# Linear attention into a swish MLP on one core: PSUM lent bank by bank, and the second batch's lead-in rearranged

## The chip, the cores and the metric

The kernel runs on one NeuronCore of one Trainium2 chip. The metric is device time in microseconds; a quoted time is the median of several executions. Each run also has a profile of one execution. The span in a profile is some 1.7 us shorter than the time of the same execution, because it goes from the first to the last instruction of the program. All runs here count as fast ones (with one core the only other label would be a run over 1.5% above the fastest).

## The reference

Two parts, one after the other, with 8 batches, 8 heads, 576 positions and head size 64:

```python
q_s = exp(q - max) / (sum over the head dimension + 1e-9)
k_s = exp(k - max) / (sum over the sequence + 1e-9)
kv  = einsum('bhsd,bhse->bhde', k_s, v)          # 64 x 64 for each head
x   = einsum('bhsd,bhde->bhse', q_s, kv)         # as 4608 tokens x 512
h   = x @ w_in                                   # 512 x 2048
g   = h * (1 / (1 + exp(-beta * h)))
out = g @ w_out                                  # 2048 x 512
```

The second part has nearly all the arithmetic: 1152 matmuls of 128x512 with a 128x128 weight, half of them for `h`, half for `out`.

## The kernel before

Tokens come in nine chunks of 512: one for each batch (its first 512 positions), and one of the eight batches' remaining 64 positions each. For a chunk, `h` is made in 16 units of four matmuls; ScalarE makes `th = tanh(beta*h/2)`, VectorE `g = (th + 1) * h`, and the second product (`acc`) takes `g` as its weight. From chunk 1 on, second-product matmuls stand between the units of the same chunk, four per unit and at least `LAG` units behind. The attention part of batch n+1 is hooked into chunk n. Batches 0 and 1 cannot be hidden so; each has a lead-in of its own, and the second lies between chunk 0 and chunk 1. For each pair of heads j, the lead-in has five `kv` matmuls, a norm (VectorE takes a reciprocal, then writes the kv blocks as `kvp`), one `x` matmul of 128x512 that needs the norm, and a copy of `x` out of PSUM. The units of `h` need all four.

```python
ldp = tc.tile_pool(name="ld", bufs=13)                 # landing buffers of all loads
psH = tc.tile_pool(name="psH", bufs=3, space=PSUM)     # h; also acc 2 and 3 of chunk 0
psB = tc.tile_pool(name="psB", bufs=2, space=PSUM)     # acc
psX = tc.tile_pool(name="psX", bufs=2, space=PSUM)     # transposes, x
psK = tc.tile_pool(name="psK", bufs=1, space=PSUM)     # kv
# [...]
def lead_in(b, fill):
    v_first(b, 0)
    v_cast(b, 0, nc.gpsimd); v_cast(b, 1, nc.gpsimd)
    v_cast(b, 2, nc.scalar); v_cast(b, 3, nc.scalar if b else nc.vector)
    fill(0)
    kv_mm(b, 0); kv_mm(b, 1)
    v_first(b, 1, 0, 1)
    v_cast(b, 4, nc.gpsimd); v_cast(b, 5, nc.scalar)
    kv_norm(b, 0, 2, nc.scalar)                        # half of it on ScalarE
    if b == 0:
        kv_mm(b, 2)
    fill(1)
    x_mm(b, 0); x_mm(b, 1)
    v_first(b, 1, 1, 2)
    v_cast(b, 6, nc.gpsimd); v_cast(b, 7, nc.scalar)
    if b:
        fill(2)
        kv_mm(b, 2)
    kv_norm(b, 2, 1, nc.vector)
    x_out(b, 0, nc.scalar); x_out(b, 1, nc.scalar)
    fill(3)
    kv_mm(b, 3)
    x_mm(b, 2)
    kv_norm(b, 3, 1, nc.vector)
    # [... x_out 2, x_mm 3, x_out 3 ...]
    for i in range(2 + b):
        unit_mm(b, i, 0, 3)                            # first three quarters of 2 or 3 units

def loads_1():
    for hf in range(2): load_q(1, hf)
    load_w_out(12); load_w_out(14)
    for hf in range(2): load_kv("k", k, 1, hf, True)
    load_kv("v", v, 1, 0, True)
    load_kv("v", v, 1, 1, True, 0, 2); load_kv("v", v, 1, 1, True, 2, 4)
    # [... batch 2 ...]

for n in range(NCH):
    for i in range(NJ):
        unit_a(n, i, 3 if n < 2 and i < 2 + n else 0)
        for f in hooks.get((n, i), []): f()
        if n:
            b_mm(2 if n == 1 and i < 4 else 4)         # up to so many second-product matmuls
    if n == 0:
        b_mm(28)
        # [... q of batch 1: exp, sum, division ...]
        cast_w_out(12, nc.scalar); cast_w_out(14, nc.scalar)
        # [... exp of k ...]
        q_t_pe(1, 0, 0, 4, nc.vector)                  # 8 transposes, copied out by VectorE
        b_mm(8)
        q_t_pe(1, 1, 0, 4, nc.vector)
        b_mm(8)
        lead_in(1, lambda m: b_mm((0, 4, 4, 4, 0)[m]))
```

So chunk 0 has 64 second-product matmuls. Of these 56 are done before chunk 1, and the last eight between its first units.

The softmax here doesn't subtract the row's maximum and nothing guards it: scores larger than these inputs give would overflow.

## Time and profile before

| | before |
|---|---|
| time at first, median of 3 | 296.31 us (296.21 to 296.71) |
| the profiled execution | 296.77 us, span 295.1 us |
| TensorE busy | 95% of the span |
| pitch of 128x512 matmuls back to back | 0.216 us |

The page of the kernel before, its span, the line of busy times (busy us, share, instructions) and the engine line of the chain that ended last (shares of the span):

```profile
span 295.1 us, 4168 instructions
...
PE 280.9 (95%) x1421; PEld 131.2 (44%) x1449; DVE 162.2 (55%) x308; ACT 172.2 (58%) x281; POOL 75.6 (26%) x129
...
PE 80%; DMA 10%; DVE 4%; POOL 2%; ACT 1%; issue 1%; POOLq 0%; ACTq 0%; DVEq 0%
```

TensorE is the bound (busy 95% of the span), so time can be saved only where TensorE has nothing to do. The timeline of TensorE, from 20 to 70 us, shows where that is (start us, duration us, engine, line, operation, out<-in, how often; in brackets the idle time before and what ended it):

```profile
20.10 11.38 PE L350 MATMUL h<-xT,w_in_b 128*128 128x512 bf16 x51 [0.42 <-DVE g L364]
31.32 6.35 PE L393 MATMUL acc<-w_out_b,g 128*128 128x512 bf16 x27
40.14 0.62 PE L200 MATMUL tp<-ident,Eq 128*128 128x128 bf16 x8 [2.47 <-POOL Eq L183]
...
45.49 0.67 PE L271 MATMUL kv<-va,Ek 128*128 128x130 bf16 x9 [0.77 <-POOL va L143]
...
51.11 0.39 PE L312 MATMUL x<-qT,kvp 128*128 128x512 bf16 x1 [0.81 <-DVE kvp L292]
51.34 2.52 PE L350 MATMUL h<-xT,w_in_b 128*128 128x512 bf16 x9
...
61.40 1.02 PE L350 MATMUL h<-xT,w_in_b 128*128 128x512 bf16 x4 [0.74 <-DVE g L364]
...
64.42 1.03 PE L350 MATMUL h<-xT,w_in_b 128*128 128x512 bf16 x4
...
68.82 0.73 PE L271 MATMUL kv<-va,Ek 128*128 128x130 bf16 x10 [0.65 <-DVE kvp L292]
```

The brackets are a little short, since the ends of matmuls are modelled (2.47 us in the second one). In this text a gap is the time from one start to the next less the usual pitch: the second bracket is then 2.6 us. Small waits are in no bracket at all. The line at 64.42 is unit 9 of chunk 1.

The wait at 45.49 names GpSimd's casts of v. GpSimd itself waited for the load, as its own timeline shows:

```profile
44.68 1.25 POOL L143 TENSOR_SCALAR_AFFINE_SELECT va<-v 128x256 bf16<-128x256 f32 x3 [4.59 <-DMA v<-in_v_dram]
```

### The profile page before, as it was taken

The numbers are of one execution on the slowest core, as the hardware profiler recorded it, in microseconds if no ns is written. First come the engines' busy times: TensorE is split into PE (matmuls) and PEld (weight loads), VectorE is DVE, ScalarE is ACT, GpSimd is POOL, SyncE is SP. The second block draws the span as 40 slices with busy tenths as digits, with TensorE's granted clock in tenths as the row PEclk, the third lists the DMA queues.
The fourth block names the chain that finished last, engine by engine and source line by source line (L and its number), as shares of the span: only waits on it lengthen the run. The fifth ranks groups of instructions, "written<-read, shape, count | busy, mean of one in ns | idle before, by whom it ended". The sixth has DMA issues, their size and how long they took to land.

```text
span 295.1 us, 4168 instructions
## 1 busy us (share of the span) xinstructions
PE 280.9 (95%) x1421; PEld 131.2 (44%) x1449; DVE 162.2 (55%) x308; ACT 172.2 (58%) x281; POOL 75.6 (26%) x129
## 2 busy tenths in 40 slices
PE   8899967989999999999999999999999999999994
PEld 3444433434445444544454445444444444444441
DVE  5848474586677556655765476548544443343300
ACT  4568475784784568556864686458554544454511
POOL 8476622180082016200621063105300000000000
PEclk9999999999999999999999999999999999999999
DMA  7999999639939962995299419921400110031111
GB/s 239 357 384 386 370 340 355 245 84 300 258 99 265 338 63 93 281 330 65 75 257 361 75 71 236 369 57 71 109 25 13 71 39 36 0 72 38 36 71 71
DMA packets 54966, 51.67 MB, mean 175 GB/s; under 512 B 21136, under 2 KB 46752, under 8 KB 54944
## 3 DMA queue, kind: packets, MB, share of 16 engines
q1 hardware_dynamic: 54912, 51.39, 58.5%
q8 instruction: 11, 0.18, 0.3%
q14 instruction: 11, 0.09, 0.1%
q10 hardware_dynamic: 32, 0.01, 0.0%
HBM read 38.28 MB, written 9.44 MB: 162 GB/s over the span
## 4 chain that ended last, share of the span: by engine, by line
PE 80%; DMA 10%; DVE 4%; POOL 2%; ACT 1%; issue 1%; POOLq 0%; ACTq 0%; DVEq 0%
PE acc L393 38%; PE h L350 36%; DMA wi<-in_moe_w_in_dram 4%; DMA q<-in_q_dram 4%; PE kv L271 3%; DMA v<-in_v_dram 3%; PE x L312 2%; DVE va L448 1%; DVE g L364 1%; ACT th L362 1%; POOL Eq L183 1%; PE warm L459 1%; DVE kvp L292 0%; DVE qz L179 0%; PE tp L200 0%
## 5 line engine op out<-in xcount | busy, mean ns | idle before, releaser
L364 DVE SCALAR_TENSOR_TENSOR g<-th,h 128x512 bf16<-128x512 bf16 x144 | 98.4, 685 | 103.1 <-ACT th L362 102.9
L362 ACT ACTIVATE th<-h,beta_h 128x512 bf16<-128x512 f32 x144 | 98.9, 688 | 93.5 <-PE h L350 91.8
L393 PE MATMUL acc<-w_out_b,g 128*128 128x512 bf16 x557 | 143.9, 379 | 0.9
L350 PE MATMUL h<-xT,w_in_b 128*128 128x512 bf16 x506 | 129.1, 379 | 1.9 <-DVE g L364 1.2
L350 PEld LDWEIGHTS <-w_in_b 128*128 128x128 bf16 x576 | 56.3, 98 | 70.1 <-issue 2.8
L393 PEld LDWEIGHTS <-g 128*128 128x128 bf16 x576 | 55.2, 98 | 63.2 <-issue 1.3
L183 POOL TENSOR_TENSOR Eq<-Eq,qz 128x512 bf16<-128x512 bf16 (+1 forms) x26 | 29.0, 1114 | 97.2 <-DVE qz L180 70.5
L410 ACT ACTIVATE o<-acc 128x512 f32<-128x512 f32 x34 | 20.3, 596 | 9.9 <-PE acc L393 9.9
L241 ACT ACTIVATE Ek<-k 128x640 bf16<-128x640 f32 (+1 forms) x28 | 22.7, 810 | 2.6 <-DMA k<-in_k_dram 2.6
L179 DVE TENSOR_REDUCE qz<-Eq 128x8 f32<-128x512 bf16 (+1 forms) x28 | 21.2, 758 | 3.6 <-ACT Eq L171 3.6
L171 ACT ACTIVATE Eq<-q 128x512 bf16<-128x512 f32 (+1 forms) x28 | 19.3, 690 | 6.5 <-DMA q<-in_q_dram 6.5
L143 POOL TENSOR_SCALAR_AFFINE_SELECT va<-v 128x256 bf16<-128x256 f32 x56 | 21.0, 414 | 7.7 <-DMA v<-in_v_dram 7.6
L350 PE MATMUL h<-xTt,w_in_b 128*128 128x512 bf16 x62 | 16.2, 379 | 0.1
L271 PE MATMUL kv<-va,Ek 128*128 128x130 bf16 x160 | 12.0, 219 | 1.5 <-POOL va L143 0.8
L271 PEld LDWEIGHTS <-Ek 128*128 128x128 bf16 x160 | 10.1, 97 | 7.0 <-issue 4.5
L312 PE MATMUL x<-qT,kvp 128*128 128x512 bf16 x32 | 11.8, 380 | 1.2 <-DVE kvp L292 0.8
L459 PE MATMUL warm<-zero 128*128 128x512 bf16 x39 | 11.3, 437 | 1.3 <-DVE zero L421 1.3
L134 ACT CAST xT<-x 128x512 bf16<-128x512 f32 (+1 forms) x20 | 10.6, 540 | 2.4 <-DVE xT L148 2.2
L148 DVE CAST xT<-x 128x512 bf16<-128x512 f32 (+1 forms) x16 | 9.9, 618 | 0.1
L225 POOL TENSOR_TENSOR Et<-Et,zt 128x512 bf16<-128x512 bf16 x4 | 4.2, 1043 | 22.3 <-ACT th L362 11.3
L292 DVE TENSOR_TENSOR kvp<-kv,rk 64x128 bf16<-64x128 f32 (+1 forms) x34 | 9.3, 273 | 0.9
L143 POOL TENSOR_SCALAR_AFFINE_SELECT w_in_b<-wi 128x1024 bf16<-128x1024 f32 (+1 forms) x9 | 8.5, 948 | 4.7 <-DMA wi<-in_moe_w_in_dram 4.7
(43 smaller groups left out, 74.2 us busy)
## 6 DMA issues: line engine op xcount, KB each, us to landing
k<-in_k_dram SPq DMA_DIRECT2D x28, 320.0 KB, 6.5
v<-in_v_dram SPq DMA_DIRECT2D x26, 320.0 KB, 7.6
q<-in_q_dram SPq DMA_DIRECT2D x16, 512.0 KB, 5.1
out_dram<-o SPq DMA_DIRECT2D x32, 256.0 KB, 2.4
wi<-in_moe_w_in_dram SPq DMA_DIRECT2D x8, 512.0 KB, 7.8
wo<-in_moe_w_out_dram SPq DMA_DIRECT2D x8, 512.0 KB, 12.2
k<-in_k_dram SPq DMA_DIRECT2D x4, 256.0 KB, 7.5
qt<-in_q_dram SPq DMA_DIRECT2D x8, 128.0 KB, 8.5
```

What stands on the lines that cost most here:

```text
L143: nc.gpsimd.affine_select(out=dst, in_=src, pattern=[[0, n]], base=0, channel_multiplier=0, compare_op=ALU.is_equal, fill=fill0,)
L171: nc.scalar.activation(Eq[b][:, :, h0:h1, :].rearrange("p t h d -> p h t d"), ld["q", b, hf][:, a : a + h1 - h0, :].rearrange("p h (t d) - ...
L179: nc.vector.tensor_reduce(qz[b][:, :, h], Eq[b][:, :, h, :], axis=AX.X, op=ALU.add)
L183: eng.tensor_tensor(Eq[b][:, t0:t1, h0:h1], Eq[b][:, t0:t1, h0:h1], qz[b][:, t0:t1, h0:h1].unsqueeze(3).to_broadcast((P, t1 - t0, h1 - h0, ...
L241: nc.scalar.activation(Ek[b][:, :, h0:h1, :].rearrange("p t h d -> p h t d"), ld["k", b, hf][:, a : a + h1 - h0, :].rearrange("p h (t d) - ...
L271: nc.tensor.matmul(kvs[b, j // 2][:, j % 2, :], Ek[b][:, t, 2 * j : 2 * j + 2, :].rearrange("p h d -> p (h d)"), va[b % 2][:, t, j, :], st ...
L312: nc.tensor.matmul(xps[b, j][:], kvp[b][:, j, :], qT[b][:, :, j, :], start=True, stop=True)
L350: nc.tensor.matmul(hs[n, i][:], w_in_b[:, kt, i * P : (i + 1) * P], rhs_a(n, kt), start=(kt == 0), stop=(kt == KT - 1),)
L362: nc.scalar.activation(th[:], h[:], ACTF.Tanh, scale=beta_h[:, i : i + 1])
L364: nc.vector.scalar_tensor_tensor(out=g[:], in0=th[:], scalar=1.0, in1=h[:], op0=ALU.add, op1=ALU.mult)
L393: nc.tensor.matmul(acc[n, st][:], gs[n, j][:, st * P : (st + 1) * P], w_out_b[:, j, :], start=(j == 0), stop=(j == NJ - 1),)
L410: nc.scalar.activation(o[:], acc[n, st][:], ACTF.Copy, scale=0.5)
```

## The change

Its intent: give each PSUM bank a name and lend it to whichever stage needs one; do more of chunk 0's second product before the transposes of batch 1 (44, then 4) and leave sixteen of them, not eight, for the first units of chunk 1; do kv of pairs 2 and 3 before the x that do not need them (`lead_in` is shared, so batch 0 gets the new order too); write norm 0 wholly on VectorE, and move a few casts and copies to another engine; and load the last quarter of w_out behind k and v of batch 1. The idle matmuls (`spare`, on zeros) take the place of useful ones in the lead-in.

```diff
-    psH = [... 3 bufs ...]  psB = [... 2 ...]  psX = [... 2 ...]  psK = [... 1 ...]
+    banks = {n: [... a pool of one bank ...] for n in ("H0", "H1", "H2", "A0", "A1", "X0", "X1", "K")}
+    def h_bank(n, i):
+        if n == 0 and i < 12:
+            return ("H0", "H1", "H2", "A0", "A1")[i % 5]
+        if n == 1 and i < 2:
+            return ("X0", "H1")[i]
+        return f"H{(n * NJ + i) % 3}"
 [... acc of chunk 0 in A0, A1, X1, K; of the others in A0, A1 ...]
-    def lead_in(b, fill):
+    def lead_in(b, kb, xb, fill):
 [...]
-        kv_norm(b, 0, 2, nc.scalar)
-        if b == 0:
-            kv_mm(b, 2)
+        v_first(b, 1, 1, 2, nc.scalar)
+        v_cast(b, 6, nc.gpsimd)
+        v_cast(b, 7, nc.scalar)
+        kv_mm(b, 2, kb[1])
+        kv_norm(b, 0, 2)
         fill(1)
-        x_mm(b, 0)
-        x_mm(b, 1)
-        [... v_first, v_cast 6 and 7, fill(2), kv_mm 2 ...]
-        kv_norm(b, 2, 1, nc.vector)
+        x_mm(b, 0, xb[0])
+        kv_mm(b, 3)
+        x_mm(b, 1, xb[1])
+        kv_norm(b, 2, 1)
         x_out(b, 0, nc.scalar)
         x_out(b, 1, nc.scalar)
-        fill(3)
-        kv_mm(b, 3)
-        x_mm(b, 2)
-        kv_norm(b, 3, 1, nc.vector)
+        fill(2)
+        x_mm(b, 2, xb[2])
+        kv_norm(b, 3, 1)
 [...]
-        for i in range(2 + b):
+        for i in range(2 - b):
             unit_mm(b, i, 0, 3)
 [... loads_1: load_w_out(12), load_w_out(14) moved behind the loads of v ...]
-                b_mm(2 if n == 1 and i < 4 else 4)
+                b_mm(0 if n == 1 and i < 1 else 4)
         if n == 0:
-            b_mm(28)
+            b_mm(44)
 [... the casts of w_out 12 and 14 moved from here (ScalarE) to behind the lead-in (GpSimd) ...]
-            q_t_pe(1, 0, 0, 4, nc.vector)
-            b_mm(8)
-            q_t_pe(1, 1, 0, 4, nc.vector)
-            b_mm(8)
-            lead_in(1, lambda m: b_mm((0, 4, 4, 4, 0)[m]))
+            q_t_pe(1, 0, nc.vector, "X0")
+            b_mm(4)
+            q_t_pe(1, 1, nc.vector, "H2")
+            spare = bank("H0", [P, CH], F32, "spare")
+            def idle_1(m):
+                for _ in range((3, 2, 1, 1)[m]):
+                    nc.tensor.matmul(spare[:], zero[:, 0:P], zero[:], start=True, stop=True)
+            lead_in(1, ("H1", "X0"), ("H2", "H1", "X0", "H2"), idle_1)
```

The parts hang together. With w_out's last quarter loaded last, none of the sixteen matmuls that need it can stand in the lead-in, so they must wait for chunk 1. And with acc 2 and 3 of chunk 0 in the h pool, as before, they cannot wait: a deadlock. By the code, the two open accumulators hold two of three h buffers while the lead-in takes three for its first units. This is what the lent banks are for, and it is why the deferral alone could not be tried on the old layout.

More of the change, by code (lines that the diff above doesn't have):

```diff
@@ L52, with bank @@
     osp = ctx.enter_context(tc.tile_pool(name="os", bufs=4))
-    psH = ctx.enter_context(tc.tile_pool(name="psH", bufs=3, space=bass.MemoryType.PSUM))
-    psB = ctx.enter_context(tc.tile_pool(name="psB", bufs=2, space=bass.MemoryType.PSUM))
-    psX = ctx.enter_context(tc.tile_pool(name="psX", bufs=2, space=bass.MemoryType.PSUM))
-    psK = ctx.enter_context(tc.tile_pool(name="psK", bufs=1, space=bass.MemoryType.PSUM))
+    banks = {
+        n: ctx.enter_context(tc.tile_pool(name=f"ps{n}", bufs=1, space=bass.MemoryType.PSUM))
+        for n in ("H0", "H1", "H2", "A0", "A1", "X0", "X1", "K")
+    }
+    def bank(n, shape, dtype, name):
+        return banks[n].tile(shape, dtype, tag=n, name=name)
     ctx.enter_context(tc.manual_schedule())
@@ L77, with xbank @@
     ld: dict = {}
+    turn = [0]
+    def xbank(n=None):
+        turn[0] ^= 1
+        return n or f"X{turn[0]}"
     def unit(name):
@@ L191, in q_t_alloc, with q_t_pe @@
         qT[b] = atn.tile([P, NT, HP, P], BF16, tag="qT", name=f"qT{b}")
-    def q_t_pe(b, hf, t0, t1, eng):
+    def q_t_pe(b, hf, eng, n=None):
         if b not in qT:
             q_t_alloc(b)
-        ps = psX.tile([P, t1 - t0, 2, P], BF16, tag="x", name=f"tp{b}_{hf}_{t0}")
-        for t in range(t0, t1):
+        ps = bank(xbank(n), [P, NT, 2, P], BF16, f"tp{b}_{hf}")
+        for t in range(NT):
             for j in range(2):
@@ L200, in q_t_pe @@
                 nc.tensor.transpose(
-                    ps[:, t - t0, j, :],
+                    ps[:, t, j, :],
                     Eq[b][:, t, h : h + 2, :].rearrange("p h d -> p (h d)"),
@@ L204, in q_t_pe @@
                 )
-        cast(eng, qT[b][:, t0:t1, 2 * hf : 2 * hf + 2, :], ps[:])
+        cast(eng, qT[b][:, :, 2 * hf : 2 * hf + 2, :], ps[:])
     def q_t_dma(b):
@@ L245, in k_exp, with v_first @@
         )
-    def v_first(b, hf, j0=0, j1=2):
-        nc.vector.tensor_scalar(
-            va[b % 2][:, 0, 2 * hf + j0 : 2 * hf + j1, 0 : 2 * D].rearrange(
-                "p j (two d) -> p j two d", two=2
-            ),
-            ld["v", b, hf][:, 2 * j0 : 2 * j1, 0:D].rearrange("p (j two) d -> p j two d", two=2),
-            even[:, 0:1], None, op0=ALU.mult,
-        )
+    def v_first(b, hf, j0=0, j1=2, eng=None):
+        dst = va[b % 2][:, 0, 2 * hf + j0 : 2 * hf + j1, 0 : 2 * D].rearrange(
+            "p j (two d) -> p j two d", two=2
+        )
+        src = ld["v", b, hf][:, 2 * j0 : 2 * j1, 0:D].rearrange("p (j two) d -> p j two d", two=2)
+        if eng is nc.scalar:
+            nc.scalar.activation(dst, src, ACTF.Copy, scale=even[:, 0:1])
+        else:
+            nc.vector.tensor_scalar(dst, src, even[:, 0:1], None, op0=ALU.mult)
     def v_cast(b, h, eng):
@@ L264, with kv_mm @@
     kvs: dict = {}
-    def kv_mm(b, j):
-        if j % 2 == 0:
-            pool, tag = (psB, "acc") if b == 0 and j else (psK, "kv")
-            kvs[b, j // 2] = pool.tile([P, 2, VW], F32, tag=tag, name=f"kv{b}_{j}")
+    def kv_mm(b, j, n="K"):
+        if (b, j // 2) not in kvs:
+            t = bank(n, [P, 2, VW], F32, f"kv{b}_{j}")
+            kvs[b, j // 2] = t
         for t in range(K5):
@@ L306, with x_mm @@
     xps: dict = {}
-    def x_mm(b, j):
+    def x_mm(b, j, n=None):
         if b not in xT:
             xT[b] = atn.tile([P, KT, NT, P], BF16, tag="xT", name=f"xT{b}")
-        xps[b, j] = psX.tile([P, NT, P], F32, tag="x", name=f"x{b}_{j}")
+        xps[b, j] = bank(xbank(n), [P, NT, P], F32, f"x{b}_{j}")
         nc.tensor.matmul(
@@ L323, in x_tail @@
     def x_tail(b, eng):
-        ps = psX.tile([P, HP, R], F32, tag="x", name=f"xt{b}")
+        ps = bank(xbank(), [P, HP, R], F32, f"xt{b}")
         i = (b % 2) * R
@@ L344 @@
     hs: dict = {}
+    def h_bank(n, i):
[4 more added lines that the diff above has]
+        return f"H{(n * NJ + i) % 3}"
     def unit_mm(n, i, k0, k1):
         if k0 == 0:
-            hs[n, i] = psH.tile([P, CH], F32, tag="h", name=f"h{n}_{i}")
+            hs[n, i] = bank(h_bank(n, i), [P, CH], F32, f"h{n}_{i}")
         for kt in range(k0, k1):
@@ L390, in b_mm @@
             if j == 0:
-                pool, tag = (psH, "h") if n == 0 and st > 1 else (psB, "acc")
-                acc[n, st] = pool.tile([P, DM], F32, tag=tag, name=f"acc{n}_{st}")
+                name = (f"A{st % 2}", ("A0", "A1", "X1", "K")[st])[n == 0]
+                acc[n, st] = bank(name, [P, DM], F32, f"acc{n}_{st}")
             nc.tensor.matmul(
@@ L453 @@
         nc.gpsimd.memset(kvp[b][:], 0.0)
-    warm = psB.tile([P, CH], F32, tag="acc", name="warm")
+    warm = bank("H2", [P, CH], F32, "warm")
     def dummy(m, n=CH):
@@ L469 @@
     k_exp(0, 4, 8)
-    q_t_pe(0, 0, 0, 4, nc.vector)
+    q_t_pe(0, 0, nc.vector)
     dummy(3)
-    q_t_pe(0, 1, 0, 4, nc.vector)
-    bt = psH.tile([P, NJ], F32, tag="h", name="bt")
+    q_t_pe(0, 1, nc.vector)
+    bt = bank("H1", [P, NJ], F32, "bt")
     nc.tensor.transpose(bt[:], beta_r[:], identf[:])
@@ L484, in lead_in @@
         v_cast(b, 2, nc.scalar)
-        v_cast(b, 3, nc.scalar if b else nc.vector)
+        v_cast(b, 3, nc.vector)
         fill(0)
-        kv_mm(b, 0)
+        kv_mm(b, 0, kb[0])
         kv_mm(b, 1)
@@ L491, in lead_in @@
         v_cast(b, 5, nc.scalar)
-        kv_norm(b, 0, 2, nc.scalar)
-        if b == 0:
-            kv_mm(b, 2)
-        fill(1)
-        x_mm(b, 0)
-        x_mm(b, 1)
-        v_first(b, 1, 1, 2)
+        v_first(b, 1, 1, 2, nc.scalar)
         v_cast(b, 6, nc.gpsimd)
         v_cast(b, 7, nc.scalar)
-        if b:
-            fill(2)
-            kv_mm(b, 2)
-        kv_norm(b, 2, 1, nc.vector)
+        kv_mm(b, 2, kb[1])
+        kv_norm(b, 0, 2)
+        fill(1)
+        x_mm(b, 0, xb[0])
+        kv_mm(b, 3)
+        x_mm(b, 1, xb[1])
+        kv_norm(b, 2, 1)
         x_out(b, 0, nc.scalar)
         x_out(b, 1, nc.scalar)
-        fill(3)
-        kv_mm(b, 3)
-        x_mm(b, 2)
-        kv_norm(b, 3, 1, nc.vector)
-        x_out(b, 2, nc.vector, 0, 2)
-        x_out(b, 2, nc.scalar, 2, 4)
+        fill(2)
+        x_mm(b, 2, xb[2])
+        kv_norm(b, 3, 1)
+        x_out(b, 2, nc.vector)
         if b == 0:
@@ L515, in lead_in @@
             cast_w_in(0, 0, nc.gpsimd, 128, 256)
-        fill(4)
-        x_mm(b, 3)
-        x_out(b, 3, nc.vector, 0, 2)
-        x_out(b, 3, nc.scalar, 2, 4)
-        for i in range(2 + b):
+        fill(3)
+        x_mm(b, 3, xb[3])
+        x_out(b, 3, nc.scalar, 0, 2)
+        x_out(b, 3, nc.vector, 2, 4)
+        for i in range(2 - b):
             unit_mm(b, i, 0, 3)
@@ L525, in loads_1 @@
             load_q(1, hf)
-        load_w_out(12)
-        load_w_out(14)
         for hf in range(2):
@@ L532, in loads_1 @@
         load_kv("v", v, 1, 1, True, 2, 4)
+        load_w_out(12)
+        load_w_out(14)
         for hf in range(2):
@@ L537, in loads_1 @@
             load_kv("v", v, 2, hf)
-    lead_in(0, lambda m: dummy((2, 3, 2, 2, 2)[m]))
+    lead_in(0, ("K", "A0"), ("X0", "X1", "A1", "H1"), lambda m: dummy((1, 3, 1, 1)[m]))
     cast_w_in(256, 0, nc.gpsimd)
@@ L589 @@
         for i in range(NJ):
-            unit_a(n, i, 3 if n < 2 and i < 2 + n else 0)
+            unit_a(n, i, 3 if n < 2 and i < 2 - n else 0)
             for f in hooks.get((n, i), []):
@@ L602 @@
             q_div(1, 0, NT, nc.vector, 4, 8)
-            cast_w_out(12, nc.scalar)
-            cast_w_out(14, nc.scalar)
             for hf in range(2):
                 k_exp(1, 4 * hf, 4 * hf + 4)
-            q_t_pe(1, 0, 0, 4, nc.vector)
-            b_mm(8)
-            q_t_pe(1, 1, 0, 4, nc.vector)
-            b_mm(8)
-            lead_in(1, lambda m: b_mm((0, 4, 4, 4, 0)[m]))
+            q_t_pe(1, 0, nc.vector, "X0")
[4 more added lines that the diff above has]
+                for _ in range((3, 2, 1, 1)[m]):
+                    nc.tensor.matmul(
+                        spare[:], zero[:, 0:P], zero[:], start=True, stop=True
+                    )
+            lead_in(1, ("H1", "X0"), ("H2", "H1", "X0", "H2"), idle_1)
+            cast_w_out(12, nc.gpsimd)
+            cast_w_out(14, nc.gpsimd)
     b_mm(10000)
```

## The prediction

> **What bounds it now.** TensorE: the page has it 95% busy, and 80% of the chain of waits. In the timeline 128x512 matmuls start every 0.216 us, and from 70 us on almost without gaps, so only the start can shrink. Its gaps there: 0.6 us at 20.1 (h waits for g: three h banks), 2.6 at 40.1 (transposes wait for the division), 0.9 at 45.5 (kv waits for cast v), 0.3 at 47.1, 1.0 at 51.1, 0.2 at 52.0 (x waits for kvp, h for x), 0.2, 0.3, 0.9 at 58 to 61.4 (h waits for g; ScalarE is behind), 0.8 at 68.8 (second kv waits for the one K bank). From 31 us on: 7.2 us.
>
> **What the change does.**
> 1. Banks. [...] Chunk 0's h gets five for units 0 to 11, then three. The gap at 20.1 goes. But h12 takes h10's bank and waits for g10, which in the trace ends 1.6 us after its h, with one unit (0.86 us) between: a new gap of 0.8 us. Lead-in 0 is about even (norm all on VectorE saves a hop, h1 waits for x3's bank). The first h stage ends near 31.6, not 31.3.
> 2. 44 second-product matmuls (9.5 us) before the transposes, not 28, end at 41.1, after the division (40.1): the 2.6 us gap is filled.
> 3. Loads. The DMA view shows 345 to 390 GB/s up to 45 us: bandwidth-bound, 1.36 us per 512 KB. [...] Two w_out units out of the way bring batch 1's last v to 43.5, not 46.2. Then VectorE's queue (q out, v, v) sets the first kv, near 44.2.
> 4. Lead-in 1. Norm 0 ends about 46.0; the other two norms follow each other on VectorE (0.66 us each), and x2 waits for both, as its bank is theirs: x2 at 48.1, h of chunk 1 at 49.2 (51.3 before). Seven idle matmuls replace sixteen useful ones here.
> 5. So eight more chunk-0 matmuls (1.7 us) are left: of 2.1 us only 0.4 is net yet. They go, four per unit, into units 1 to 4 of chunk 1, where ScalarE (tanh 0.69 + exp 0.62 us per unit) starved TensorE: the 1.4 us of gaps at 58 to 61 and that at 52 should close. Net at unit 9, where both have done 73 second-product matmuls: 62.4 against 64.4.
> 6. Afterwards the same work in the same order; the gap at 68.8 stays. Moved copies and casts cost nothing.
>
> **Sum.** 2.0 us saved. Predicted **294.2 us**, 8 in 10 within **293.2 to 295.3**. Faster by over 2%: 0.01; within 2%: 0.98; slower: 0.01.
>
> **What would show it.** Right: no TensorE gap at 40; one of 0.8 before h12 near 28; last v near 43.5; a gap under 1.5 us before x2; none above 0.3 between units 1 and 9 of chunk 1; all after 70 shifted by 2 us. Wrong: v not earlier, TensorE waiting for GpSimd's casts in lead-in 1, or h waiting for g in chunk 1.
>
> **What would make it wrong.** The first h stage losing or gaining more; the kv, norm, x chain of lead-in 1 being longer; w_out's casts too late for units 1 to 4; ScalarE still behind in chunk 1.

## The result, and the profile after

| | before | after |
|---|---|---|
| time, median | 296.26 us (4 runs) | 294.65 us (4 runs) |
| ratio | | 0.9947 (95%: 0.993 to 0.9964) |
| the same again, later (chip 11) | 296.15 us (11 runs) | 294.60 us (6 runs), 0.9939 (0.9917 to 0.996) |
| the profiled execution | 296.77 us, span 295.1 us | 294.75 us, span 293.0 us |

A ratio is taken over the fast runs of both kernels in the same rounds, so it is not quite the ratio of the medians. The change saves 1.6 us by the medians, 0.5%. That is within 2%, as the prediction had it with 0.98, and clear of noise, since the interval ends at 0.9964. The two profiled executions differ by 2.0 us, mainly because that of before was itself 0.5 us slower than its median.

The page after, the same lines:

```profile
span 293.0 us, 4194 instructions
...
PE 283.7 (97%) x1453; PEld 131.7 (45%) x1453; DVE 162.0 (55%) x309; ACT 168.9 (58%) x274; POOL 77.4 (26%) x131
...
PE 82%; DMA 14%; DVE 2%; issue 1%; ACT 0%; POOL 0%; SPq 0%; ACTq 0%; POOLq 0%
```

TensorE's timeline after, from 20 to 70 us:

```profile
28.17 3.61 PE L368 MATMUL h<-xT,w_in_b 128*128 128x512 bf16 x16 [0.64 <-DVE g L382]
31.62 9.66 PE L411 MATMUL acc<-w_out_b,g 128*128 128x512 bf16 x44
41.12 0.61 PE L210 MATMUL tp<-ident,Eq 128*128 128x128 bf16 x8
...
44.31 1.01 PE L282 MATMUL kv<-va,Ek 128*128 128x130 bf16 x15 [0.63 <-DVE va L265]
...
48.05 0.39 PE L323 MATMUL x<-qT,kvp 128*128 128x512 bf16 x1 [1.02 <-DVE kvp L303]
...
49.23 1.89 PE L368 MATMUL h<-xT,w_in_b 128*128 128x512 bf16 x8 [0.35 <-DVE xT L158]
...
62.39 1.03 PE L368 MATMUL h<-xT,w_in_b 128*128 128x512 bf16 x4
...
66.79 0.73 PE L282 MATMUL kv<-va,Ek 128*128 128x130 bf16 x10 [0.66 <-DVE kvp L303]
```

Unit 9 of chunk 1 starts at 62.39 instead of 64.42; as many second-product matmuls (73) have been done by then in both. After that the two run alike. All that TensorE lost between 16 us and 70 us, in gaps as defined above:

| where | before | after |
|---|---|---|
| chunk 0: start of its units (17 to 20 us) | 0.8 | 0.4 |
| chunk 0: unit 12 (28 us) | 0 | 0.8 |
| first second-product matmuls (32 us) | 0.15 | 0 |
| transposes wait for the division (40 us) | 2.6 | 0 |
| first kv | 0.9 | 0.8 |
| x0 waits for norm 0 | 0.3 | 0.3 |
| the last x wait for norms 2 and 3 | 1.0 | 1.2 |
| h of chunk 1 waits for x | 0.2 | 0.5 |
| h waits for g (58 to 61 us) | 1.5 | 0 |
| second kv of batch 2 | 0.8 | 0.8 |
| idle matmuls in lead-in 1 | 0 | 1.5 |
| sum | 8.2 | 6.3 |

The sums differ by 1.9 us; h of chunk 0 starting at 16.58 and not 16.73 makes it 2.0. This table says where TensorE stood still. It does not say which part of the change is worth what, since a gap that is filled in one place can just be a later start in another. That is what the experiments are for.

VectorE's timeline after shows what now sets lead-in 1: the copy of the second transpose, then the v instructions (the two waited-for ones are the lines at 43.68 and 44.18), and later two norms in a row (46.64 to 48.00), for which x2 at 48.05 waits:

```profile
43.08 0.69 DVE L158 COPY qT<-tp 128x1024 bf16<-128x1024 bf16 x1 [0.62 <-PE tp L210]
43.68 0.58 DVE L265 TENSOR_SCALAR va<-v,even 128x256 bf16<-128x256 f32 x1
44.18 0.28 DVE L158 CAST va<-v 128x256 bf16<-128x256 f32 x1
...
46.64 0.17 DVE L293 RECIPROCAL rk<-kv 128x1 f32<-128x1 f32 x1 [0.77 <-PE kv L282]
46.85 0.46 DVE L303 TENSOR_TENSOR kvp<-kv,rk 64x64 bf16<-64x64 f32 x2
47.34 0.17 DVE L293 RECIPROCAL rk<-kv 128x1 f32<-128x1 f32 x1
47.54 0.46 DVE L303 TENSOR_TENSOR kvp<-kv,rk 64x64 bf16<-64x64 f32 x2
```

GpSimd's casts of v, for comparison with the line of before (44.68), begin 2.5 us earlier:

```profile
42.13 0.75 POOL L153 TENSOR_SCALAR_AFFINE_SELECT va<-v 128x256 bf16<-128x256 f32 x2 [1.83 <-DMA v<-in_v_dram]
```

### The profile page after: what moved, and what is told of

Its sections match the earlier page's. It is cut to its first block, busy times and chain, and to the rows that moved or that the text cites. A ratio compares the mean times of both kernels' runs of the same rounds, so it can differ in the third digit from the quotient of the medians.

```text
span 293.0 us, 4194 instructions
## 1 busy us (share of the span) xinstructions
PE 283.7 (97%) x1453; PEld 131.7 (45%) x1453; DVE 162.0 (55%) x309; ACT 168.9 (58%) x274; POOL 77.4 (26%) x131
## 4 chain that ended last, share of the span: by engine, by line
PE 82%; DMA 14%; DVE 2%; issue 1%; ACT 0%; POOL 0%; SPq 0%; ACTq 0%; POOLq 0%
PE acc L411 39%; PE h L368 37%; DMA v<-in_v_dram 5%; DMA wo<-in_moe_w_out_dram 4%; DMA wi<-in_moe_w_in_dram 3%; PE kv L282 3%; PE x L323 2%; DMA q<-in_q_dram 2%; DVE kvp L303 1%; POOL va L153 0%; PE xt L338 0%; DVE xT L158 0%; ACT th L380 0%; DVE g L382 0%; DVE rk L293 0%
## 5 line engine op out<-in xcount | busy, mean ns | idle before, releaser
L411 PE MATMUL acc<-w_out_b,g 128*128 128x512 bf16 x576 | 145.9, 379 | 0.0
L144 ACT CAST xT<-x 128x512 bf16<-128x512 f32 (+1 forms) x18 | 9.9, 557 | 5.7 <-PE x L323 5.7
L303 DVE TENSOR_TENSOR kvp<-kv,rk 64x128 bf16<-64x128 f32 (+1 forms) x36 | 9.9, 274 | 0.9
```

The costliest lines, as they stand in the source:

```text
L411: nc.tensor.matmul(acc[n, st][:], gs[n, j][:, st * P : (st + 1) * P], w_out_b[:, j, :], start=(j == 0), stop=(j == NJ - 1),)
```

## The experiments

The theory is that of the prediction: the chain division, transpose, copy, kv, norm, x sets the start of chunk 1, the load order keeps data out of this chain, and deferred matmuls fill TensorE where ScalarE is behind. Its rivals: the gain is the filled gap at 40 us; or the loads alone; or the order of pairs. All twelve kernels gave correct results. Edits are against the changed kernel if nothing else is said. A difference in us is between medians; kernels of different calls ran on different chips, and the ratio to the kernel before of the same rounds is given for each.

| run | median us | ratio to before (95%) |
|---|---|---|
| after_again | 294.60 | 0.9939 (0.9917 to 0.996) |
| e1_old_load_order | 295.41 | 0.9972 (0.9959 to 0.9984) |
| e2_no_idle | 295.58 | 0.997 (0.9942 to 0.9997) |
| e3_h12_bank | 293.82 | 0.9917 (0.9903 to 0.993) |
| e5_x2_bank | 293.96 | 0.9915 (0.99 to 0.993) |
| e6_useful_fill | 293.18 | 0.9894 (0.988 to 0.9907) |
| e7_two_per_unit | 293.99 | 0.992 (0.9907 to 0.9934) |
| e8_no_deferral | 294.89 | 0.9951 (0.993 to 0.9972) |
| e12_old_pair_order | 295.16 | 0.9968 (0.9939 to 0.9996) |
| e13_v_before_copy | 293.90 | 0.9919 (0.9896 to 0.9942) |
| c1_all_three | 292.00 | 0.985 (0.9832 to 0.9869) |
| c2_all_four | 291.85 | 0.9844 (0.982 to 0.9869) |

### after_again: the changed kernel once more

No edit; it gives a value on the chip of the last three experiments, and a look at how often its clock dips.

> The changed kernel once more, on the chip of the three runs beside it, so that they are compared on one chip: about 294.65 us; runs with a mean granted clock of 0.994 or less, if any, some 1.6 us longer.

Measured: 294.60 us; 294.43 to 294.83 in six executions, all with a mean granted clock of 0.998 or more.

### e1_old_load_order: is it the loads?

```diff
         for hf in range(2):
             load_q(1, hf)
+        load_w_out(12)
+        load_w_out(14)
 [... k, v ...]
-        load_w_out(12)
-        load_w_out(14)
```

> The changed kernel with only the load order of before (w_out's last quarter ahead of k, v of batch 1; casts stay behind the lead-in). Theory (the first kv of batch 1 is set by v's landing in this order): last v lands near 46.3 us instead of 43.6, first kv waits for GpSimd's cast of v, the chain of lead-in 1 is 1.4 us later, time about 296.05 us, +1.4 on the changed kernel. Rival (the order of matmuls and the banks made the whole gain; the loads are hidden): within 0.3 us of the changed kernel.

Measured: 295.41 us, 0.8 us more than the changed kernel. The mechanism is the expected one: in TensorE's timeline the kv now wait for GpSimd's casts.

```profile
44.05 0.22 PE L282 MATMUL kv<-va,Ek 128*128 128x130 bf16 x1 [0.40 <-DVE va L265]
44.94 0.95 PE L282 MATMUL kv<-va,Ek 128*128 128x130 bf16 x14 [0.68 <-POOL va L153]
```

The size was little more than half. The expectation took the landing times from the changed kernel's profile. In this execution all loads came earlier: the first half of q of batch 1 landed at 34.66 us, against 35.63 in the changed kernel's profile (landing times are read from the traces' transfer records). The same load landed at 35.42, 35.45, 35.05 and 34.85 in the profiles of before, e3, e6 and e7. Every slice of before's DMA view from 3 to 45 us has the DMA engines nine tenths busy or more. A landing time 30 us into such a start moved by a microsecond from one execution to another (34.66 to 35.63 us), and an estimate that adds a wait to one landing time inherits that.

### e3_h12_bank: the new gap at unit 12

```diff
         if n == 0 and i < 12:
             return ("H0", "H1", "H2", "A0", "A1")[i % 5]
+        if n == 0:
+            return ("H2", "H0", "H1", "H2")[i - 12]
```

> The changed kernel with units 12 to 15 of chunk 0 on banks H2, H0, H1, H2, so that unit 12 no longer takes the bank of unit 10. Theory: the 0.8 us gap before h12 goes, and since lead-in 1 is set by TensorE's and VectorE's queue and not by data, all of it reaches the end: about 293.9 us, -0.75. Rival (v's landing sets lead-in 1): the gain is eaten by a longer wait before the first kv, within 0.2 us of the changed kernel.

Measured: 293.82 us, 0.8 us less than the changed kernel; the gap is gone and the second product starts at 30.85 instead of 31.62. In this profile the h units of chunk 0 run through, with no bracket:

```profile
26.75 4.26 PE L370 MATMUL h<-xT,w_in_b 128*128 128x512 bf16 x19
30.85 2.32 PE L413 MATMUL acc<-w_out_b,g 128*128 128x512 bf16 x10
```

All of it reached the end, so v's landing did not set lead-in 1. This entry of the bank table costs 0.8 us for no gain.

### e6_useful_fill: is the filled gap at 40 us the gain?

```diff
-            b_mm(44)
+            b_mm(37)
 [...]
-                for _ in range((3, 2, 1, 1)[m]):
-                    nc.tensor.matmul(spare[:], zero[:, 0:P], zero[:], start=True, stop=True)
+                b_mm((3, 2, 1, 1)[m])
```

> The changed kernel with 37 instead of 44 second-product matmuls before the transposes, and the other seven in place of the seven idle ones. Theory: what counts is when the chain division, transpose, copy, kv, norm, x starts; a gap of about 0.75 us opens again before the transposes, the transposes start at 40.35 instead of 41.12 and all of chunk 1 comes 0.75 us earlier: about 293.9 us. Rival (filling the gap at 40 us was the gain): the reopened gap costs, +0.7 us or no change at best.

Measured: 293.18 us, 1.5 us less. Seven matmuls at 0.216 us are 1.5 us, and the chain came 1.2 us (transposes) to 1.4 us (kv, h) earlier. TensorE's timeline of this run, against 41.12, 44.31 and 49.23 in the changed kernel:

```profile
39.92 0.61 PE L210 MATMUL tp<-ident,Eq 128*128 128x128 bf16 x8
...
42.88 1.01 PE L282 MATMUL kv<-va,Ek 128*128 128x130 bf16 x15 [0.40 <-DVE va L265]
...
47.79 1.46 PE L368 MATMUL h<-xT,w_in_b 128*128 128x512 bf16 x6 [0.35 <-DVE xT L158]
```

The expected 0.75 us of reopened gap did not appear, as q had landed 0.6 us earlier in this execution (35.05 us) and the division was over in time. So the run shows one thing: work moved ahead of the transposes is not gained when it delays them. With 44, the changed kernel overfills: it puts work before the transposes, and idle matmuls behind them. It does not put the rival out, since with 37 the gap at 40 us stayed filled: what the other nine additional matmuls are worth there was not tried, and no run leaves the gap open in the new layout.

### e7_two_per_unit: does chunk 1 need four deferred matmuls per unit?

```diff
-                b_mm(0 if n == 1 and i < 1 else 4)
+                b_mm((0 if i < 1 else 2 if i < 9 else 4) if n == 1 else 4)
```

> The changed kernel with two second-product matmuls per unit instead of four in units 1 to 8 of chunk 1. Theory (the deferred matmuls fill the time in which ScalarE starves TensorE): gaps before h with waits for g come back in units 4 to 9, together about 0.9 us (0.5 to 1.4), and TensorE's total grows by that: about 295.5 us. Rival (ScalarE is not behind any more, since the lead-in is shorter): no gaps, within 0.2 us of the changed kernel.

Measured: 293.99 us, 0.65 us less, where 0.9 us more was expected. One small gap (0.17 us) came into the units; and the gap before the second kv of batch 2, 0.8 us in the changed kernel and in before, fell to 0.08:

```profile
63.00 0.73 PE L282 MATMUL kv<-va,Ek 128*128 128x130 bf16 x10
63.56 1.03 PE L411 MATMUL acc<-w_out_b,g 128*128 128x512 bf16 x4
64.43 1.03 PE L368 MATMUL h<-xT,w_in_b 128*128 128x512 bf16 x4
65.37 0.74 PE L282 MATMUL kv<-va,Ek 128*128 128x130 bf16 x10
```

In the changed kernel the sixteen are used up after unit 4. At the kv only one second-product matmul is far enough behind (`LAG`) to be let in, and one unit and one matmul do not cover the norm that the second kv waits for. With two per unit, some are still there: four stand between the two kv groups, and the norm is covered. So two per unit are enough for ScalarE, and the rest is worth more later.

### e8_no_deferral: eight deferred, as before, instead of sixteen

Against e1_old_load_order (w_out must be there early for this):

```diff
+            cast_w_out(12, nc.gpsimd)
+            cast_w_out(14, nc.gpsimd)
 [... right behind the division; the same two lines behind the lead-in are gone ...]
-                [... idle matmuls (3, 2, 1, 1) ...]
+                b_mm((3, 2, 1, 2)[m])
 [...]
-                b_mm(0 if n == 1 and i < 1 else 4)
+                b_mm(2 if n == 1 and i < 4 else 4)
```

> The kernel of e1_old_load_order (295.41 us) with w_out's last casts early and eight more chunk-0 matmuls in place of its idle ones in lead-in 1, so that eight and not sixteen are left for chunk 1, two per unit in units 0 to 3 as in the kernel before. Theory (deferred matmuls are what fills TensorE while ScalarE is behind): 1.7 us of work is done in waits that were idle, but gaps before h with waits for g come back in units 4 to 8 of chunk 1, 1.0 us or more together: -0.3 us against e1, between -0.7 and +0.2. Rival (the shorter lead-in alone removed the starving, and the deferral does nothing): no such gaps, -1.5 us.

Measured: 294.89 us (ratio 0.9951, e1 0.9972), 0.5 us less than e1: inside the range of the theory, but not for the reason given. Only one gap came back:

```profile
59.24 1.02 PE L368 MATMUL h<-xT,w_in_b 128*128 128x512 bf16 x4 [0.20 <-DVE g L382]
```

That is 0.36 us, not the 1.0 or more expected. In its profile v landed later than in that of e1 (kv waited 1.26 us for GpSimd's cast, against 0.84), which took 0.4 us of the 1.7 us back; another 0.29 us went between the first four h and the second product at 51.33. What is left, 0.7 us, is the difference of the two profiled executions (294.62 and 295.33 us). One of its six executions had a clock of 0.994. So the comparison is good for this much: without the deferral ScalarE starves TensorE far less than in the kernel before (1.5 us), so most of that starving had gone for another reason. ScalarE's timelines suggest which. Before, its first tanh of chunk 1 came 2.55 us after the first h matmul (53.89 after 51.34), since three units' first quarters stood ahead; in the changed kernel it came 1.05 us after (50.28 after 49.23), with one unit ahead. First before:

```profile
53.89 0.69 ACT L362 ACTIVATE th<-h,beta_h 128x512 bf16<-128x512 f32 x1 [1.52 <-PE h L350]
```

Then after:

```profile
50.28 0.69 ACT L380 ACTIVATE th<-h,beta_h 128x512 bf16<-128x512 f32 x1 [1.00 <-PE h L368]
```

In e8, which also has one unit ahead, it came 1.34 us after (51.52 after 50.18). This is read from the traces and not tried alone.

### e2_no_idle: what do the idle matmuls do?

```diff
-                for _ in range((3, 2, 1, 1)[m]):
-                    nc.tensor.matmul(spare[:], zero[:, 0:P], zero[:], start=True, stop=True)
+                pass
```

> The changed kernel without the seven idle matmuls in lead-in 1. Theory: each of them stands in a wait that VectorE sets, so TensorE just waits longer in the same places: within 0.25 us of the changed kernel (294.65 us). Rival (they keep the clock up): the granted clock falls below 1.0 in the record and chunk 1 starts slower, over 1 us longer. Second rival (they are in the way): 0.4 us or more faster.

Measured: 295.58 us, with two kinds of executions: 294.48, 294.58 and 295.03 us at a mean granted clock of 1.0, and 296.13, 296.26 and 296.93 us at 0.994, 0.994 and 0.988. The profile fell on one of the second kind. The view of stretches has, for each, its length, the busy time of TensorE (count), weight loads, VectorE, ScalarE, GpSimd, then the granted clock, DMA share and GB/s. First without the idle matmuls:

```profile
45.90:49.30 3.40, 1.60 (x11) 0.69 (x10) 2.24 (x8) 1.46 (x3) 0.91 (x1) 1.00 1.08 352
49.30:52.70 3.40, 3.40 (x10) 1.23 (x9) 0.72 (x2) 1.51 (x3) 0.00 (x0) 0.50 1.07 363
```

Then the changed kernel:

```profile
45.90:49.30 3.40, 2.00 (x12) 0.88 (x13) 1.92 (x7) 1.46 (x3) 1.18 (x2) 1.00 1.05 347
49.30:52.70 3.40, 3.40 (x17) 1.51 (x17) 1.71 (x3) 2.42 (x5) 0.00 (x0) 1.00 1.07 361
```

For 3.4 us, just as chunk 1 starts, the granted clock is 0.50: the view counts ten matmuls there, and seventeen in the changed kernel. The first eight h of chunk 1 and the four second-product matmuls after them take 4.27 us (49.03 to 53.30), against 2.58 in the changed kernel (49.23 to 51.81), so the timeline loses 1.7 us to it. In the 3.4 us before the drop TensorE was busy for 1.60 us, in the same stretch of the changed kernel for 2.00. Why only three of the six executions of e2 were hit was not shown. At least at the start the moment of change is not fixed by the program: the traces' records of the full clock begin at 5.10 us in before and at 6.98 us in after, and the first weight loads come every 0.43 us up to 5.07 and 6.78 us, and then about every 0.2 us. One stretch of 3.4 us at 0.50 in a span of 294.5 us makes a mean clock of 0.994, and two would make 0.988: the values seen above (that the execution at 0.988 had two is an estimate from these numbers, as it has no profile). So the first theory fell. The idle matmuls cost nothing in good executions (294.5 to 295.0 us without them, 294.4 to 294.8 with them) and save some 1.7 us in the others. They are insurance: three of six executions had a clock of 0.994 or less without them, none of ten with them. Useful matmuls in their places (e6, c1) seem to give the same protection: none of the four executions of each dipped. It is not full protection: e8, with useful ones, and e12, with idle ones, each had one execution of six at 0.994.

### e5_x2_bank: x2 waits for a bank

```diff
-            lead_in(1, ("H1", "X0"), ("H2", "H1", "X0", "H2"), idle_1)
+            lead_in(1, ("H1", "X0"), ("H2", "H1", "H0", "H2"), idle_1)
-                for _ in range((3, 2, 1, 1)[m]):
+                for _ in range((3, 2, 1, 0)[m]):
```

> The changed kernel with x2 of batch 1 in bank H0, so that it does not wait for the norm of pair 3 to leave its bank (the idle matmul after it is dropped). Theory: x2 starts 0.7 us earlier, its copy 0.4 us earlier, h of chunk 1 reaches its fourth part 0.5 us earlier: about 294.15 us, -0.5. Rival (x2 is not the last wait; the chain ends with x3 and VectorE's queue all the same): within 0.2 us of the changed kernel.

Measured: 293.96 us, 0.7 us less. In the table of banks, x2 of batch 1 is put where kv of pairs 2 and 3 lies, and so waits for both norms. In another bank it waits for norm 2 alone; the first three parts of h follow x3 at once:

```profile
47.06 0.39 PE L323 MATMUL x<-qT,kvp 128*128 128x512 bf16 x1 [0.32 <-DVE kvp L303]
47.76 0.39 PE L323 MATMUL x<-qT,kvp 128*128 128x512 bf16 x1 [0.30 <-DVE kvp L303]
47.98 0.87 PE L368 MATMUL h<-xT,w_in_b 128*128 128x512 bf16 x3
```

### e12_old_pair_order: kv of pairs 2 and 3 ahead of x

For batch 1 only, back to the old order:

```diff
+            kv_norm(b, 0, 2)
+            fill(1)
+            x_mm(b, 0, xb[0])
+            x_mm(b, 1, xb[1])
+            kv_mm(b, 2, kb[1])
+            kv_norm(b, 2, 1)
+            [... x_out 0 and 1 ...]
+            fill(2)
+            kv_mm(b, 3)
+            x_mm(b, 2, xb[2])
+            kv_norm(b, 3, 1)
```

> The changed kernel with lead-in 1 in the old order: x0 and x1 first, then kv of pair 2, its norm, kv of pair 3. Theory: the norm of pair 3 can follow that of pair 2 at once only if both kv are there; in the old order kv 3 waits for norm 2, so x2 (which waits for both norms) comes about 0.6 us later: about 295.2 us, +0.6. Rival (the order of the pairs is hidden behind VectorE's queue): within 0.2 us.

Measured: 295.16 us, 0.55 us more (and one execution of six at a clock of 0.994, 296.83 us). VectorE's timeline has the reason: norm 3 waits for its kv instead of following norm 2 (in the changed kernel 47.34 follows 46.85 without a wait).

```profile
46.68 0.46 DVE L303 TENSOR_TENSOR kvp<-kv,rk 64x64 bf16<-64x64 f32 x2
47.69 0.17 DVE L293 RECIPROCAL rk<-kv 128x1 f32<-128x1 f32 x1 [0.55 <-PE kv L282]
```

### e13_v_before_copy: what sets the first kv?

```diff
             b_mm(4)
+            v_first(1, 0)
+            v_cast(1, 3, nc.vector)
             q_t_pe(1, 1, nc.vector, "H2")
 [... and the two left out of lead_in for batch 1 ...]
```

> The changed kernel with VectorE's first two v instructions of batch 1 ahead of the copy of the second transpose in its queue. Theory (VectorE's queue, not the data, sets the first kv and norm 0): first kv near 43.5 instead of 44.3, norm 0 and everything after it 0.7 us earlier: about 293.95 us. Rival (v's landing or GpSimd's casts set it): within 0.2 us.

Measured: 293.90 us, 0.7 us less than after_again in the same rounds. The first kv starts at 43.44 us, right behind the idle matmuls, and norm 0 is written at 44.41; in the profile of after_again these came at 44.20 and 45.17, both 0.76 us later. VectorE's timeline:

```profile
42.29 0.34 DVE L265 TENSOR_SCALAR va<-v,even 128x256 bf16<-128x256 f32 x1
42.55 0.28 DVE L158 CAST va<-v 128x256 bf16<-128x256 f32 x1
42.99 0.69 DVE L158 COPY qT<-tp 128x1024 bf16<-128x1024 bf16 x1 [0.16 <-PE tp L210]
```

With the new load order it is the queue of VectorE, not the data, that sets lead-in 1. Together with e1 this closes the question of the loads: they had to be moved for data to drop out of the chain.

### c1_all_three and c2_all_four: what helped, together

c1 has the bank tables of e3 and e5, `b_mm(40)` ahead of the transposes, `b_mm((2, 1, 1, 0)[m])` for the idle matmuls, and e7's two per unit. c2 adds the move of e13.

> All that has helped, on the changed kernel: unit 12's bank, x2's bank, 40 second-product matmuls ahead of the transposes and four useful ones in place of the idle ones, two per unit in units 1 to 8 of chunk 1. Theory: the parts add except that the transposes cannot start before the division ends (39.7 to 40.3 us): -0.8 to -1.4 from the chain's start, -0.5 from x2, -0.6 from the spread: about 292.4 us, between 291.9 and 293.0. Rival (one wait is behind the others): not below e6_useful_fill, 293.2 us.

Measured: 292.00 us, 2.6 us less than the changed kernel and 0.985 of the kernel before. This beats both kernels.

> c1_all_three (292.0 us) with the same move on VectorE. Theory: another 0.5 to 0.7 us, about 291.4 us, if v has landed by then (c1's chain is a microsecond earlier than the changed kernel's, and v lands at 41.5 to 42.0). Rival (now v's landing sets the first kv): 292.0 us, no change.

Measured: 291.85 us, ratio 0.9844 against 0.985. The times alone do not separate the two answers, since the intervals cover both. The traces speak for the rival: h of chunk 1 starts at 46.47 us, in c1 at 46.49, although in c2 the transposes began 0.26 us later (39.81, after a wait for the division). With the chain a microsecond and a half earlier, data are back in it. TensorE's timeline of c2 waits for GpSimd's casts again, and GpSimd for v:

```profile
42.56 1.10 PE L282 MATMUL kv<-va,Ek 128*128 128x130 bf16 x14 [0.33 <-POOL va L153]
```

## Why the prediction was right

The measured time (294.65 us) lies in the range, near the point (294.2).

- **First h stage.** Predicted: the gap at 20.1 goes, one of 0.8 comes before h12 near 28, the stage ends near 31.6. Measured: 0.80 at 28.17, end at 31.62. e3 shows that this gap reaches the end in full.
- **44 before the transposes.** Predicted end 41.1, transposes at once; measured 41.12. But 44 were too many: e6 moved seven of them behind the transposes and gained 1.5 us. What the filled gap itself is worth was not tried.
- **Loads.** Predicted last v at 43.5 and first kv near 44.2, set by VectorE's queue; measured 43.60 and 44.31. (The view's slices from 3 to 45 us run from 294 to 389 GB/s, a wider range than the prediction names.) e1 shows that the order of loads is worth 0.8 us, and e13 that VectorE's queue is what sets the first kv afterwards.
- **Lead-in 1.** Predicted x2 at 48.1 and h at 49.2; measured 48.05 and 49.23. e5 shows the bank that x2 waits for, e12 that having kv of pairs 2 and 3 early is worth 0.55 us.
- **Chunk 1.** Predicted no gaps and unit 9 at 62.4; measured none and 62.39. The reason was put too simply. The eight more deferred matmuls were said to be what closes ScalarE's 1.4 us; e7 shows that two per unit do as well, and e8 that without them 0.36 us comes back. The trace suggests that ScalarE simply starts earlier, relative to h. So the 62.4 was met although one of its reasons did little of the work, and that is in part luck.
- **The idle matmuls.** The prediction counted them as a plain loss of 1.5 us. Without them three of e2's six executions had a clock of 0.994 or less; of the changed kernel's ten none did. They are a loss only because useful matmuls could stand there (e6).
- **Size.** Predicted 2.0 us saved; 2.0 between the two profiled executions, 1.6 between the medians. The sum was taken from a profile of an execution that was 0.5 us slower than the median of its kernel, which is probably why it came out 0.4 us too large.

What stays open. Of the 32 executions of the kernel before that ran beside the experiments, six had a mean granted clock of 0.994 or less, and took 297.0 to 297.8 us. None of the changed kernel's ten did. The long gap at 40 us is a candidate, but the profile of before is of an execution without a dip, and ten executions are too few to say that the change cured it. From 36.73 to 40.14 us TensorE was busy for 0.94 of 3.41 us in that profile, less than the 1.60 of 3.40 us before the drop in e2; that such a stretch can bring on a dip was not shown. Such executions explain part of a small ratio: by the means, after_again stands at 0.9937 with the three of the kernel before in its rounds, and at 0.9948 without them. Several parts of the change were not tried alone: the filled gap at 40 us, five banks for the first units of chunk 0, one instead of three units begun ahead in lead-in 1, and the moved norms and casts.

## What to carry to other kernels

When the bounding engine waits for a chain of small steps on other engines, a gap that gets filled is not yet time gained: ask whether the chain starts earlier, and put the fill inside the chain's waits, and not so much of it ahead of the first step that this step is delayed. When banks or buffers are given out by hand, check for each that its last user is far enough back; two entries of this table cost 0.8 and 0.7 us. Idle matmuls in a long wait may be holding the clock (without them three of e2's six executions had one of 0.994 or less, and took some 1.7 us longer), so replace them with useful ones rather than delete them.
